# Restructuring the first tile of a six-layer cross network: x0 transposed by batch block, layer 0 begun on four accumulators

## The chip, the cores and the metric

The kernel runs on one core of a Trainium2 chip. The metric is the device time of one execution in microseconds (us), lower is better. The kernel before takes 2669.94 us (median of 4 runs, 2669.66 to 2670.76).

The engines are called PE (TensorE: matmuls and transposes), DVE (VectorE), ACT (ScalarE), POOL (GpSimd) and SP (SyncE, which issues the loads). The traces show PE at two speeds: a 512-column matmul starts every 427 ns or every 216 ns, a 128-column transpose every 107 or every 56 ns. The **gate** below is a name for this alone: it opens where the spacing falls to 216 and 56 ns (at 11.97 us in the trace of the kernel before), and it shuts where 427 and 107 ns come back. 427 beside 216 ns is called half clock.

## The reference, cut to what matters

```python
# B, Din, L = 16384, 1024, 6; all bf16
def reference(x0, ws, bs):
    x = x0
    for l in range(L):
        proj = jnp.einsum('bd,de->be', x, ws[l]) + bs[l]
        x = x0 * proj + x
    return x
```

## The kernel before

The batch is cut into 32 tiles of 512 rows. In a tile, x lies transposed (feature on the partitions). Each layer is 8 output blocks `e` of 8 matmuls over `k`, so 64 matmuls a layer and 12,288 in all. A PSUM accumulator `ps[e]` lives through all six layers; after each layer one DVE operation makes `(ps + c) * x0T`. All tiles but the first get their transposed x0 by a transposing load. In the first tile x0 is loaded as it lies, transposed on PE into PSUM and copied to `x0T` by DVE.

```python
load_x0n(0, 256)        # x0 of tile 0 in four column pieces of 256 KB (512 B rows)
load_w0(0, 128)         # layer 0's weights in column pieces
load_x0n(256, 512)
load_x0n(512, 768)
load_x0n(768, 1024)
load_w0(128, 256)
load_w0(256, 512)
load_w0(512, 1024)
for l2 in range(1, L):
    nc.sync.dma_start(out=w_sb[l2], in_=ws_v[l2])     # 2 MB each
...                      # 5 warm-up matmuls on a zeroed tile, one small transpose of bs
# first tile, first layer, e == 0
for kp in range(KT // 2):
    for k in (2 * kp, 2 * kp + 1):
        tp = psum.tile([P, NB], BF16, name="tp", tag=f"ps{1 + k % 5}")
        for bo in range(BO):                          # 4 transposes per k
            nc.tensor.transpose(tp[:, bo*P:(bo+1)*P], x0n[:, bo, k*P:(k+1)*P], ident)
        nc.vector.tensor_copy(out=x0T[:, k, :], in_=tp)
    if kp == 0:
        make_c()
    for k in (2 * kp, 2 * kp + 1):
        mm(ps[0], l, e, k, cur)                       # only block e = 0 starts here
...                      # then e = 1..7, eight matmuls each
```

Of the kernel before, what the change touches and what calls it, by code (L numbers as in the profile page):

```python
# [8 lines left out]
BF16 = mybir.dt.bfloat16  # L9
FP32 = mybir.dt.float32  # L10
ADD = mybir.AluOpType.add
MULT = mybir.AluOpType.mult

N_WARM = 5


@with_exitstack
def kernel(
    ctx: ExitStack,
    tc: tile.TileContext,  # L20
    x0: bass.AP,
    ws: bass.AP,
    bs: bass.AP,
    out: bass.AP,
):
    nc = tc.nc
    P = nc.NUM_PARTITIONS
    B, D = x0.shape
    L = ws.shape[0]
    KT = D // P  # L30
    NB = 512
    NT = B // NB
    BO = NB // P

    wpool = ctx.enter_context(tc.tile_pool(name="w", bufs=1))
    cpool = ctx.enter_context(tc.tile_pool(name="c", bufs=1))
    x0pool = ctx.enter_context(tc.tile_pool(name="x0", bufs=3))
    xpool = ctx.enter_context(tc.tile_pool(name="x", bufs=3))
    opool = ctx.enter_context(tc.tile_pool(name="o", bufs=2))
    psum = ctx.enter_context(  # L40
        tc.tile_pool(name="psum", bufs=1, space=bass.MemoryType.PSUM)
    )

    def x0_nat(t):
        return x0[t * NB : (t + 1) * NB, :].rearrange("(bo bi) d -> bi bo d", bi=P)

    def out_nat(t):
        return out[t * NB : (t + 1) * NB, :].rearrange("(bo bi) e -> bi bo e", bi=P)

    w_sb = [wpool.tile([P, KT, D], BF16, name=f"w{l}") for l in range(L)]  # L50
    ws_v = [ws[l].rearrange("(ko ki) e -> ki ko e", ki=P) for l in range(L)]

    warm = cpool.tile([P, NB], BF16, name="warm")
    nc.vector.memset(warm, 0.0)  # L54
    ident = cpool.tile([P, P], BF16, name="ident")
    make_identity(nc, ident)

    bs_nat = cpool.tile([L * KT, P], BF16, name="bs_nat")
    nc.scalar.dma_start(out=bs_nat, in_=bs.rearrange("l (eo ei) -> (l eo) ei", ei=P))

    x0n = opool.tile([P, BO, D], BF16, name="o_nat")
    x0_t0 = x0_nat(0)

    def load_x0n(c0, c1):
        nc.sync.dma_start(out=x0n[:, :, c0:c1], in_=x0_t0[:, :, c0:c1])  # L65

    def load_w0(c0, c1):
        nc.sync.dma_start(out=w_sb[0][:, :, c0:c1], in_=ws_v[0][:, :, c0:c1])  # L68

    load_x0n(0, 256)  # L70
    load_w0(0, 128)
    load_x0n(256, 512)
    load_x0n(512, 768)
    load_x0n(768, 1024)
    load_w0(128, 256)
    load_w0(256, 512)
    load_w0(512, 1024)
    for l2 in range(1, L):
        nc.sync.dma_start(out=w_sb[l2], in_=ws_v[l2])

    wps = psum.tile([P, NB], FP32, name="wps", tag="ps7")
    for _ in range(N_WARM):
        nc.tensor.matmul(  # L83
            wps, lhsT=warm[:, 0:P], rhs=warm, start=True, stop=True,
            skip_group_check=True,
        )

    bsT = psum.tile([P, L * KT], BF16, name="bsT", tag="ps6")
    nc.tensor.transpose(bsT, bs_nat, ident[: L * KT, : L * KT])  # L89
    c_sb = cpool.tile([P, L, KT], FP32, name="c_sb")  # L90

    def make_c():
        nc.vector.tensor_scalar_add(c_sb[:, 0, :], bsT[:, 0:KT], 1.0)  # L93
        for l in range(1, L):
            nc.vector.tensor_add(  # L95
                c_sb[:, l, :], c_sb[:, l - 1, :], bsT[:, l * KT : (l + 1) * KT]
            )

    def mm(ps_e, l, e, k, cur):
        nc.tensor.matmul(  # L100
            ps_e,
            lhsT=w_sb[l][:, k, e * P : (e + 1) * P],
            rhs=cur[:, k, :],
            start=(l == 0 and k == 0),
            stop=(k == KT - 1),
            skip_group_check=True,
        )

    def stt(nxt, ps_e, l, e, x0T):
        nc.vector.scalar_tensor_tensor(  # L110
            out=nxt[:, e, :],
            in0=ps_e,
            scalar=c_sb[:, l, e : e + 1],
            in1=x0T[:, e, :],
            op0=ADD,
            op1=MULT,
        )

    for t in range(NT):
        x0T = x0pool.tile([P, KT, NB], BF16, name="x0T")  # L120
        ps = [None] * KT
        cur = x0T
        if t > 0:
            nc.sync.dma_start_transpose(out=x0T, in_=x0[t * NB : (t + 1) * NB, :])
        for l in range(L):
            nxt = xpool.tile([P, KT, NB], BF16, name="xT")
            for e in range(KT):
                if l == 0:
                    if t == 0 and e == 0:
                        ps[0] = psum.tile([P, NB], FP32, name="ps0", tag="ps0")  # L130
                        for kp in range(KT // 2):
                            for k in (2 * kp, 2 * kp + 1):
                                tp = psum.tile(
                                    [P, NB], BF16, name="tp", tag=f"ps{1 + k % 5}"
                                )
                                for bo in range(BO):
                                    nc.tensor.transpose(  # L137
                                        tp[:, bo * P : (bo + 1) * P],
                                        x0n[:, bo, k * P : (k + 1) * P],
                                        ident,  # L140
                                    )
                                nc.vector.tensor_copy(out=x0T[:, k, :], in_=tp)  # L142
                            if kp == 0:
                                make_c()
                            for k in (2 * kp, 2 * kp + 1):
                                mm(ps[0], l, e, k, cur)
                        stt(nxt, ps[e], l, e, x0T)
                        continue
                    ps[e] = psum.tile([P, NB], FP32, name=f"ps{e}", tag=f"ps{e}")
                for k in range(KT):  # L150
                    mm(ps[e], l, e, k, cur)
                stt(nxt, ps[e], l, e, x0T)
            cur = nxt

        o_nat = opool.tile([P, BO, D], BF16, name="o_nat")
        n_dma = KT if t < NT - 1 else KT - 2
        for e in range(n_dma):
            nc.sync.dma_start_transpose(
                out=o_nat[:, :, e * P : (e + 1) * P], in_=cur[:, e, :]
            )  # L160
        nc.sync.dma_start(
            out=out_nat(t)[:, :, 0 : n_dma * P], in_=o_nat[:, :, 0 : n_dma * P]
        )
        if n_dma < KT:
            for i, e in enumerate(range(n_dma, KT)):
                tp = psum.tile([P, BO, P], BF16, name="tpo", tag=f"ps{i}")
                for bo in range(BO):
                    nc.tensor.transpose(  # L168
                        tp[:, bo, :], cur[:, e, bo * P : (bo + 1) * P], ident
                    )  # L170
                dst = o_nat[:, :, e * P : (e + 1) * P]
                if e == KT - 1:
                    nc.vector.tensor_copy(out=dst, in_=tp)  # L173
                else:
                    nc.scalar.copy(out=dst, in_=tp)  # L175
            nc.sync.dma_start(
                out=out_nat(t)[:, :, n_dma * P : D], in_=o_nat[:, :, n_dma * P : D]
            )
# [30 lines left out]
```

## Time and profile before

| what | value | where to read it |
|---|---|---|
| span | 2668.6 us | page, first line |
| PE busy | 100% | page, part 1 |
| full-speed matmul spacing | 216 ns | timeline, start times |
| layer 1's first matmul | 24.77 us | timeline |
| 64 matmuls of layer 0 at full speed | 13.8 us | 64 x 0.216 |

These are lines of the page of the kernel before: the chain that ended last, by engine and by line, and the costliest groups (busy us, mean ns of one, idle time before them and what ended it).

```profile
PE 100%; DMA 0%; DVE 0%; SPq 0%; issue 0%
...
L100 PE MATMUL ps<-xT,w 128*128 128x512 bf16 x10240 | 2215.3, 379 | 0.0
...
L137 PE MATMUL tp<-ident,o_nat 128*128 128x128 bf16 x32 | 4.7, 305 | 2.5 <-DMA o_nat<-in_x_dram 2.5
```

PE is the whole chain, and once the stream of matmuls runs nothing interrupts it. A restructured start can therefore win only what lies ahead of layer 1. The timeline shows that stretch. Its columns are start in us, length in us, engine, line, operation, count, and the idle time before it with its releaser; lines of PE alone are kept. (Some traces below lack a few matmul records, so a count there can be 62 where 64 ran.)

```profile
1.19 2.31 PE L83 MATMUL wps<-warm 128*128 128x512 bf16 x5 [1.19 <-DVE warm L54]
...
4.12 1.03 PE L137 MATMUL tp<-ident,o_nat 128*128 128x128 bf16 x8 [0.46 <-DMA o_nat<-in_x_dram]
...
7.20 0.40 PE L137 MATMUL tp<-ident,o_nat 128*128 128x128 bf16 x2 [2.05 <-DMA o_nat<-in_x_dram]
...
7.38 1.06 PE L100 MATMUL ps<-x0T,w 128*128 128x512 bf16 x2
...
12.22 12.71 PE L100 MATMUL ps<-x0T,w 128*128 128x512 bf16 x58
...
24.77 7.50 PE L100 MATMUL ps<-xT,w 128*128 128x512 bf16 x34
```

The first 8 transposes run at 4.12 us, then PE waits 2.05 us for the second x0 piece. The two matmuls at 7.38 us take 1.06 us to their end, so they start 427 ns apart: half clock. The 58 at 12.22 us take 12.71 us, which is 216 ns each. The gate opened at 11.97 us; that is where the trace's record of the granted clock begins. A warning about reading it: where the record has not begun, the page and the table of stretches print a clock of 1.00, so the spacing of the matmuls is the safer witness.

### The profile page before, as it was taken

To read this page: it belongs to the slowest core of one execution; us is meant where nothing else is said; L and a number is where in the kernel's file an instruction comes from. 1 tells how busy PE (TensorE), PEld (TensorE's weight loads), DVE (VectorE), ACT (ScalarE), POOL (GpSimd) and SP (SyncE) were. 2 spreads that over 40 slices of the span, in tenths; PEclk is the share of its full clock that TensorE was granted. 3 is DMA by queue.
4 is the path that set the end of the run, shared out by engine and by line. 5 is a ranking of instruction groups with operands and counts; after the bars stand their busy time and mean duration, and the time that the engine had idled before them with its cause. 6 is when DMAs were issued, how large, how long until landed. Compare 5 with 4: busy or idle time off the path is not lost.

```text
span 2668.6 us, 26965 instructions
## 1 busy us (share of the span) xinstructions
PE 2660.2 (100%) x12334; PEld 1207.0 (45%) x12334; DVE 1157.9 (43%) x1552; ACT 1.9 (0%) x2; POOL 0.7 (0%) x6
## 2 busy tenths in 40 slices
PE   9999999999999999999999999999999999999999
PEld 4444444444444444444444444444444444444444
DVE  4444444444444444444444444444444444444444
ACT  0000000000000000000000000000000000000000
POOL 0000000000000000000000000000000000000000
PEclk9999999999999999999999999999999999999999
DMA  8111011110111101111011110111101111011111
GB/s 237 48 48 31 20 46 48 48 43 9 44 48 48 48 7 42 48 48 48 9 39 48 48 48 12 36 48 48 48 14 34 48 48 48 16 32 48 32 32 28
DMA packets 295217, 114.75 MB, mean 43 GB/s; under 512 B 268992, under 2 KB 274112, under 8 KB 295104
## 3 DMA queue, kind: packets, MB, share of 16 engines
q1 hardware_dynamic: 295040, 113.02, 16.7%
q8 instruction: 96, 1.57, 0.2%
q14 instruction: 17, 0.14, 0.0%
q10 hardware_dynamic: 64, 0.01, 0.0%
HBM read 13.64 MB, written 33.55 MB: 18 GB/s over the span
## 4 chain that ended last, share of the span: by engine, by line
PE 100%; DMA 0%; DVE 0%; SPq 0%; issue 0%
PE ps L100 99%; DMA o_nat<-in_x_dram 0%; PE tp L137 0%; DVE xT L110 0%; SPq L68 0%; SPq L65 0%; DVE o_nat L173 0%; PE tpo L168 0%
## 5 line engine op out<-in xcount | busy, mean ns | idle before, releaser
L100 PE MATMUL ps<-xT,w 128*128 128x512 bf16 x10240 | 2215.3, 379 | 0.0
L100 PEld LDWEIGHTS <-w 128*128 128x128 bf16 x12288 | 1202.6, 98 | 1448.9
L110 DVE SCALAR_TENSOR_TENSOR xT<-ps,c_sb,x0T 128x512 bf16<-128x512 f32 x1536 | 1153.0, 751 | 1498.2 <-PE ps L100 1498.2
L100 PE MATMUL ps<-x0T,w 128*128 128x512 bf16 x2048 | 449.3, 380 | 0.0
L137 PE MATMUL tp<-ident,o_nat 128*128 128x128 bf16 x32 | 4.7, 305 | 2.5 <-DMA o_nat<-in_x_dram 2.5
L137 PEld LDWEIGHTS <-o_nat 128*128 128x128 bf16 x32 | 3.6, 141 | 4.6 <-DMA o_nat<-in_x_dram 2.9
L142 DVE COPY x0T<-tp 128x512 bf16<-128x512 bf16 x8 | 3.4, 425 | 4.9 <-PE tp L137 4.9
L83 PE MATMUL wps<-warm 128*128 128x512 bf16 x5 | 2.3, 629 | 1.2 <-DVE warm L54 1.2
L175 ACT ACT_TABLE_LOAD x1 | 1.3, 1283 | 2505.2 <-DMA out_dram<-o_nat 2505.2
L83 PEld LDWEIGHTS <-warm 128*128 128x128 bf16 x5 | 0.6, 134 | 2.0 <-DVE warm L54 1.2
L168 PE MATMUL tpo<-ident,xT 128*128 128x128 bf16 x8 | 0.8, 220 | 0.6 <-DVE xT L110 0.6
L93 DVE TENSOR_SCALAR c_sb<-bsT 128x8 f32<-128x8 bf16 x1 | 0.2, 167 | 2.6 <-PE bsT L89 2.6
L168 PEld LDWEIGHTS <-xT 128*128 128x128 bf16 x8 | 0.5, 98 | 1.0 <-DVE xT L110 0.8
L95 DVE TENSOR_TENSOR c_sb<-c_sb,bsT 128x8 f32<-128x8 f32 x5 | 0.8, 158 | 0.1
L175 ACT COPY o_nat<-tpo 128x512 bf16<-128x512 bf16 x1 | 0.6, 586 | 157.0 <-PE tpo L168 157.0
L54 DVE MEMSET warm<- 128x256 uint32 x1 | 0.3, 272 | 0.9 <-PEq L193 0.9
L173 DVE COPY o_nat<-tpo 128x512 bf16<-128x512 bf16 x1 | 0.4, 425 | 0.5 <-PE tpo L168 0.5
L89 PEld LDWEIGHTS <-bs_nat 48*128 48x128 bf16 x1 | 0.1, 100 | 0.8 <-DMA bs_nat<-in_bs_dram 0.8
masks.py:199 POOL TENSOR_SCALAR_AFFINE_SELECT ident<-ident 128x128 bf16<-128x128 bf16 x1 | 0.3, 294 | 0.1
L89 PE MATMUL bsT<-ident,bs_nat 48*128 48x48 bf16 x1 | 0.2, 218 | 0.0
masks.py:197 POOL MEMSET ident<- 128x128 bf16 x1 | 0.2, 205 | 0.3 <-POOLq L193 0.3
L193 POOL MEMSET const-bfloat16-1.0<- 128x1 bf16 x1 | 0.1, 102 | 0.0
(3 smaller groups left out, 0.3 us busy)
## 6 DMA issues: line engine op xcount, KB each, us to landing
out_dram<-o_nat SPq DMA_DIRECT2D x31, 1024.0 KB, 6.0
w<-in_ws_dram SPq DMA_DIRECT2D x5, 2048.0 KB, 19.5
o_nat<-xT SPq DMA_TRANSPOSE x254, 2.4
o_nat<-in_x_dram SPq DMA_DIRECT2D x4, 256.0 KB, 5.5
w<-in_ws_dram SPq DMA_DIRECT2D x1, 1024.0 KB, 8.3
out_dram<-o_nat SPq DMA_DIRECT2D x1, 768.0 KB, 3.6
w<-in_ws_dram SPq DMA_DIRECT2D x2, 256.0 KB, 5.1
w<-in_ws_dram SPq DMA_DIRECT2D x1, 512.0 KB, 7.2
```

The lines of the kernel that those rows point to most:

```text
L54: nc.vector.memset(warm, 0.0)
L83: nc.tensor.matmul(wps, lhsT=warm[:, 0:P], rhs=warm, start=True, stop=True, skip_group_check=True,)
L89: nc.tensor.transpose(bsT, bs_nat, ident[: L * KT, : L * KT])
L93: nc.vector.tensor_scalar_add(c_sb[:, 0, :], bsT[:, 0:KT], 1.0)
L95: nc.vector.tensor_add(c_sb[:, l, :], c_sb[:, l - 1, :], bsT[:, l * KT : (l + 1) * KT])
L100: nc.tensor.matmul(ps_e, lhsT=w_sb[l][:, k, e * P : (e + 1) * P], rhs=cur[:, k, :], start=(l == 0 and k == 0), stop=(k == KT - 1), skip_gr ...
L110: nc.vector.scalar_tensor_tensor(out=nxt[:, e, :], in0=ps_e, scalar=c_sb[:, l, e : e + 1], in1=x0T[:, e, :], op0=ADD, op1=MULT,)
L137: nc.tensor.transpose(tp[:, bo * P : (bo + 1) * P], x0n[:, bo, k * P : (k + 1) * P], ident,)
L142: nc.vector.tensor_copy(out=x0T[:, k, :], in_=tp)
L168: nc.tensor.transpose(tp[:, bo, :], cur[:, e, bo * P : (bo + 1) * P], ident)
L173: nc.vector.tensor_copy(out=dst, in_=tp)
L175: nc.scalar.copy(out=dst, in_=tp)
```

## The change

The intent is to have PE transpose each batch block of x0 as it lands (four loads with 2 KB rows), and then to run half of layer 0, four output blocks, with `k` outermost, so that each transposed `k` feeds four matmuls. The warm-up reads a constant that exists already, so it starts earlier and has six matmuls. The weights' first half comes in quarters.

```diff
-N_WARM = 5
+N_WARM = 6
-    load_x0n(0, 256)
-    load_w0(0, 128)
-    load_x0n(256, 512)
 ... (the other column loads go too)
+    for bo in range(BO):
+        nc.sync.dma_start(out=x0n[:, bo, :], in_=x0_t0[:, bo, :])
+    for kp in range(KT // 2):
+        nc.sync.dma_start(
+            out=w_sb[0][:, 2 * kp : 2 * kp + 2, 0:H],
+            in_=ws_v[0][:, 2 * kp : 2 * kp + 2, 0:H],
+        )
+    nc.sync.dma_start(out=w_sb[0][:, :, H:D], in_=ws_v[0][:, :, H:D])
 ... (warm-up matmuls read constant ones in place of a zeroed tile)
+                        for bo in range(BO - 1):
+                            for k in range(KT):
+                                tr(k, bo)
+                        tr_last(0)           # last block's transposes and the copies
+                        tr_last(2)
 ...
+                        for k in range(KT):
+                            if k % 2 == 0 and k + 4 < KT:
+                                tr_last(k + 4)
+                            for e2 in range(EH):            # EH = 4
+                                mm(ps[e2], l, e2, k, cur)
+                        for e2 in range(EH):
+                            stt(nxt, ps[e2], l, e2, x0T)
```

In the built program the scheduler puts all 32 transposes ahead of the first matmul.

More of the change, by code (lines that the diff above doesn't have):

```diff
@@ L51 @@
     ws_v = [ws[l].rearrange("(ko ki) e -> ki ko e", ki=P) for l in range(L)]
-    warm = cpool.tile([P, NB], BF16, name="warm")
-    nc.vector.memset(warm, 0.0)
     ident = cpool.tile([P, P], BF16, name="ident")
@@ L62 @@
     x0_t0 = x0_nat(0)
-    def load_x0n(c0, c1):
-        nc.sync.dma_start(out=x0n[:, :, c0:c1], in_=x0_t0[:, :, c0:c1])
-    def load_w0(c0, c1):
-        nc.sync.dma_start(out=w_sb[0][:, :, c0:c1], in_=ws_v[0][:, :, c0:c1])
-    load_x0n(0, 256)
-    load_w0(0, 128)
-    load_x0n(256, 512)
-    load_x0n(512, 768)
-    load_x0n(768, 1024)
-    load_w0(128, 256)
-    load_w0(256, 512)
-    load_w0(512, 1024)
+    H = D // 2
+    for bo in range(BO):
[6 more added lines that the diff above has]
+    nc.sync.dma_start(out=w_sb[0][:, :, H:D], in_=ws_v[0][:, :, H:D])
     for l2 in range(1, L):
         nc.sync.dma_start(out=w_sb[l2], in_=ws_v[l2])
-    wps = psum.tile([P, NB], FP32, name="wps", tag="ps7")
+    wps = psum.tile([P, NB], FP32, name="wps", tag="ps2")
+    ones_w = nc.const_aps.tensor(1.0, [P, P], BF16)
+    ones_x = nc.const_aps.tensor(1.0, [P, NB], BF16)
     for _ in range(N_WARM):
         nc.tensor.matmul(
-            wps, lhsT=warm[:, 0:P], rhs=warm, start=True, stop=True,
+            wps, lhsT=ones_w, rhs=ones_x, start=True, stop=True,
             skip_group_check=True,
         )
-    bsT = psum.tile([P, L * KT], BF16, name="bsT", tag="ps6")
+    bsT = psum.tile([P, L * KT], BF16, name="bsT", tag="ps3")
     nc.tensor.transpose(bsT, bs_nat, ident[: L * KT, : L * KT])
@@ L128, with tr, tr_last @@
                 if l == 0:
-                    if t == 0 and e == 0:
-                        ps[0] = psum.tile([P, NB], FP32, name="ps0", tag="ps0")
-                        for kp in range(KT // 2):
-                            for k in (2 * kp, 2 * kp + 1):
-                                tp = psum.tile(
-                                    [P, NB], BF16, name="tp", tag=f"ps{1 + k % 5}"
-                                )
-                                for bo in range(BO):
-                                    nc.tensor.transpose(
-                                        tp[:, bo * P : (bo + 1) * P],
-                                        x0n[:, bo, k * P : (k + 1) * P],
-                                        ident,
-                                    )
-                                nc.vector.tensor_copy(out=x0T[:, k, :], in_=tp)
-                            if kp == 0:
-                                make_c()
-                            for k in (2 * kp, 2 * kp + 1):
-                                mm(ps[0], l, e, k, cur)
-                        stt(nxt, ps[e], l, e, x0T)
+                    if t == 0 and e < KT // 2:
+                        if e > 0:
+                            continue
+                        EH = KT // 2
+                        make_c()
+                        tps = [
+                            psum.tile(
+                                [P, 2, NB], BF16, name=f"tp{kp}", tag=f"ps{EH + kp}"
+                            )
+                            for kp in range(KT // 2)
+                        ]
+                        def tr(k, bo):
+                            nc.tensor.transpose(
+                                tps[k // 2][:, k % 2, bo * P : (bo + 1) * P],
+                                x0n[:, bo, k * P : (k + 1) * P],
+                                ident,
+                            )
+                        def tr_last(k):
+                            tr(k, BO - 1)
+                            tr(k + 1, BO - 1)
+                            for k2 in (k, k + 1):
+                                nc.vector.tensor_copy(
+                                    out=x0T[:, k2, :], in_=tps[k2 // 2][:, k2 % 2, :]
+                                )
+                        for bo in range(BO - 1):
[4 more added lines that the diff above has]
+                        for e2 in range(EH):
+                            ps[e2] = psum.tile(
+                                [P, NB], FP32, name=f"ps{e2}", tag=f"ps{e2}"
+                            )
+                        for k in range(KT):
[3 more added lines that the diff above has]
+                                mm(ps[e2], l, e2, k, cur)
+                        for e2 in range(EH):
+                            stt(nxt, ps[e2], l, e2, x0T)
```

## The prediction

> **What bounds the kernel now.** TensorE (PE). The page shows PE busy 100% and the chain of waits is 99% layer matmuls. The timeline shows them starting every 215.9 ns; 12,288 of them are 2,653 us of the 2,668.6 us span. No other engine or DMA queue bounds the steady state, and the change leaves it alone. Only the start can move: layer 1's first matmul starts at 24.77 us (timeline), while layer 0's 64 matmuls need 64 x 0.2159 = 13.8 us. So 10.95 us is start-up. The tail after the last matmul (5.5 us) is untouched.
>
> **Where the 10.95 us goes (timeline).** The first x0 piece lands at 4.07 us. PE then does 8 transposes, one each 107 ns, and waits 2.05 us for the second x0 piece (7.15 us). After that it runs 24 transposes and 8 matmuls without idling, but matmuls start 427 ns apart and transposes 107 ns apart until about 11.97 us, where the granted-clock record begins; then 216 and 56 ns. [...]
>
> **What the change does.**
> - x0 comes as four 2 KB-row pieces ahead of any weight. Packets in the trace: 512 B take 28 ns, 1,024 B 48, 2,048 B 84. So 256 KB in 2 KB rows takes about 0.67 us instead of 0.9. The first load's fixed part is about 2.4 us (12 KB of bs: 2.44 us from issue to landing). Estimate: landings at 3.8, 4.5, 5.2, 5.9 us; weight quarters (1 KB rows, 0.77 us each) at 6.6 to 9.0; second half of w0 near 12; w1 near 17.5.
> - PE: 6 warm matmuls instead of 5, starting about 0.3 us earlier (no memset), ending near 3.5 us; then 32 transposes by batch block, all ahead of the first matmul, then 32 matmuls k-outer over four accumulators, each k (0.86 us) covering two copies (0.425 us each), so DVE keeps up.
> - Adds nothing to PE but one warm matmul, hidden behind the first landing. Four evictions (0.75 us) come in a burst; layer 1 needs them 7 us later.
>
> **On the critical path.** The 2 us DMA gap goes; slow-clock time shrinks because PE is nearly continuously busy from 0.9 us. Two cases:
> - gate opens near 5.2 us: transposes finish with the last x0 piece, first real matmul about 6.8, layer 1 about 20.6; gain 4.1 us.
> - gate opens near 8.6 us: transposes end 7.2, first matmul 7.3 at 427 ns, layer 1 about 21.8; gain 3.0 us.
> Even odds, less 0.2 us for late landings (the trace has a slow DMA spell near 4 to 5 us): gain 3.3 us.
>
> **Predicted time: 2666.6 us, 8 in 10 between 2665.2 and 2668.4.** Faster by over 2%: 0.005; within 2%: 0.99; slower by over 2%: 0.005.
>
> **What would show it.** Timeline: layer 1's first matmul at 20.6 to 21.8 us; all x0 landed by about 6 us; PE gaps over 0.3 us gone after 4 us; start spacing 216 ns from between 5 and 8.6 us; steady spacing and tail unchanged; w1 landed before layer 1.
>
> **What would make it wrong.** The gate opening only near 12 us again (gain about 1.5); x0 or the first weight quarter landing over 1 us late, so PE idles; evictions in a burst stalling layer 1; a different gate phase in each run.

The two opening times of the cases, 5.2 and 8.6 us, stand as assumptions. The terms of the sum are all there: the mean of 4.1 and 3.0 us, less 0.2, put down as 3.3 us.

## The result, and the profile after

The changed kernel takes 2667.73 us (median of 9 runs, 2667.23 to 2669.68) beside 2669.94 us (13 runs, 2669.02 to 2671.03). The ratio is 0.9993, with a 95% interval of 0.9984 to 1.0002. Ratios here are the mean time of one kernel's runs over that of the other's in the same rounds, so they are not quite the ratio of the quoted medians. By the 2% rule the two are the same. The interval of the ratio holds 1 in every comparison of this document, so what follows rests on traces and on how the runs lie.

The profiled runs of the two kernels took 2670.76 and 2667.53 us, 3.23 us apart. The first is the highest of the four runs at hand before the change, 0.82 us over their median, so this pair shows more than the 2.21 us between the medians. The timeline of the changed kernel shows where (same columns as above).

```profile
0.78 2.72 PE L79 MATMUL wps<-const-bfloat16-1.0 128*128 128x512 bf16 x6 [0.78 <-PEq L213]
...
3.58 1.37 PE L138 MATMUL tp<-ident,o_nat 128*128 128x128 bf16 x16
...
5.45 0.62 PE L138 MATMUL tp<-ident,o_nat 128*128 128x128 bf16 x8 [0.50 <-DMA o_nat<-in_x_dram]
...
6.91 0.62 PE L138 MATMUL tp<-ident,o_nat 128*128 128x128 bf16 x8 [0.84 <-DMA o_nat<-in_x_dram]
7.24 2.74 DVE L148 COPY x0T<-tp 128x512 bf16<-128x512 bf16 x8 [2.41 <-PE tp L138]
...
7.71 13.97 PE L96 MATMUL ps<-x0T,w 128*128 128x512 bf16 x64 [0.18 <-DVE x0T L148]
...
21.52 10.74 PE L96 MATMUL ps<-xT,w 128*128 128x512 bf16 x49
```

The 64 matmuls now run without a break and at full speed, and layer 1 starts at 21.52 us, 3.25 us earlier. But the first real matmul starts at 7.71 us, **0.33 us later** than before (7.38). The same shows in the page's groups:

```profile
L96 PE MATMUL ps<-xT,w 128*128 128x512 bf16 x10240 | 2215.4, 379 | 0.0
...
L138 PE MATMUL tp<-ident,o_nat 128*128 128x128 bf16 x32 | 2.6, 237 | 1.3 <-DMA o_nat<-in_x_dram 1.3
```

The steady stream did not change (2215.3 and 2215.4 us). The transposes' busy time fell from 4.7 to 2.6 us, at the same count: most of them ran at full clock.

A ledger makes this exact. In every trace the span minus the start of layer 1 is 2643.9 us, so the whole difference between kernels lies ahead of layer 1. That start is the first real matmul, plus 13.82 us for 64 matmuls, plus 0.056 us for each transpose that stands between them, plus what the slow clock and waits add:

| trace | gate opens (us) | last x0 piece lands | first real matmul | transposes after it | slow clock and waits after it | layer 1 starts |
|---|---|---|---|---|---|---|
| before | 11.97 | 8.97 | 7.38 | 22: 1.23 | 2.34 | 24.77 |
| after | 4.25 | 6.87 | 7.71 | 0 | 0 | 21.52 |

So the 3.25 us are 2.34 us of slow clock, plus 1.23 us of transposes that no longer stand between matmuls, less 0.33 us of later start. PE's waits for x0 shrank from 2.5 to 1.3 us (the two groups of transposes above), but the first real matmul, which now stands behind all 32 transposes, came no earlier. The slow-clock term agrees with an estimate from the spacings: PE was busy at half clock from 7.2 to 11.97 us, and at 427 ns in place of 216 about half of that time, 4.77 x 0.5 = 2.4 us, is lost.

The last x0 piece landed at 6.87 us, where the prediction had 5.9. The view of the transfers cuts 2 to 7 us into 40 slices; first the kernel before:

```profile
GB/s 8 12 154 168 219 309 336 318 316 305 307 301 289 293 289 305 279 244 207 178 180 188 238 283 291 303 254 262 254 262 246 258 320 324 320 324 297 297 307 307
```

and the changed kernel:

```profile
GB/s 180 49 0 328 410 360 442 361 459 377 442 360 377 197 328 279 393 197 311 328 377 360 147 148 197 172 229 287 279 279 262 246 344 279 279 311 344 361 312 279
```

The changed kernel moves 360 to 459 GB/s at 2.5 to 3.5 us and 384 to 388 from 13.6 us on (table of stretches), but 147 to 287 from 4.75 to 6 us. In the same spell of both kernels single packets take up to 0.9 us (changed) and 1.4 us (before), where the medians are 84 ns (2 KB) and 27 ns (512 B). I call it the slow spell. The packet records, in which the first tile's x0 can be told by its 2 KB, show that a few packets come late and not the whole stream: of the 512 packets of x0, 500 had ended by 5.74 us, near the predicted 5.9, but the last one at 6.51 us, when 250 packets of weights had ended too. In e1 below the same times are 5.98 and 7.48 us. In both traces the landing follows that last packet by 0.36 us.

### The profile page after: what moved, and what is told of

It is laid out like the page before. It is cut to its first block, busy times and chain, and to the rows that moved or that the text cites. A ratio compares the mean times of both kernels' runs of the same rounds, so it can differ in the third digit from the quotient of the medians.

```text
span 2665.4 us, 26968 instructions
## 1 busy us (share of the span) xinstructions
PE 2658.3 (100%) x12335; PEld 1205.8 (45%) x12335; DVE 1157.1 (43%) x1551; ACT 1.9 (0%) x2; POOL 0.7 (0%) x6
## 4 chain that ended last, share of the span: by engine, by line
PE 100%; DMA 0%; DVE 0%; SPq 0%; issue 0%
PE ps L96 100%; DMA o_nat<-in_x_dram 0%; SPq L65 0%; DVE xT L106 0%; DVE x0T L148 0%; DVE o_nat L193 0%; PE tpo L188 0%; PE tp L138 0%
## 5 line engine op out<-in xcount | busy, mean ns | idle before, releaser
L96 PE MATMUL ps<-xT,w 128*128 128x512 bf16 x10240 | 2215.4, 379 | 0.0
```

What stands on the lines that cost most here:

```text
L96: nc.tensor.matmul(ps_e, lhsT=w_sb[l][:, k, e * P : (e + 1) * P], rhs=cur[:, k, :], start=(l == 0 and k == 0), stop=(k == KT - 1), skip_gr ...
```

## The experiments

Each of the 12 runs was profiled and timed in five rounds against the kernel before; all results were correct. Jobs ran on different chips, so a run is compared with those of its own job. Layer 1's start, the gate and landings are of the one profiled run; the medians are of five runs. The theories:

- **A**: the change wins mostly because PE's gate opens earlier, and the spread between runs is the moment at which it opens, which differs from run to run.
- **B** (rival, for the spread): late landings of x0 make it.
- **C** (rival, for the gain): the new order of loads, transposes and accumulators is what wins.
- **D**: the change starts its first real matmul no earlier because a whole megabyte of x0 and a weight quarter must land first.

### e1, e8, e10: the changed kernel again

No edit.

> The changed kernel unaltered, for the spread and a second trace. Theory A (the clock gate of TensorE is what the change mostly wins on[...]): runs fall into an early group near 2667.2 to 2667.8 us (gate open between 4.2 and 5.0 us) and a late group of 2668.5 us and more (a trace of such a run shows matmuls 427 ns apart after 7.7 us, or the gate closing in the waits at 5 and 6 us). Rival B (the landing of the x0 pieces makes the spread): every trace has the gate open before 5.5 us and the late runs have the last x0 piece landing 1 to 2 us later. Median 2667.7 under both.

> The changed kernel again, beside the other three on the same chip. By theory A its time is that of the gate: a trace with the gate open once for good by 5 us gives 2667.2 to 2668 us, one in which it closes again in the waits gives 2669 us or more.

> The changed kernel beside e9 on the same chip: 2667.5 to 2669.5 us, by the gate; its last x0 block lands at 6.8 to 7.9 us.

Measured: 2669.25 us (2667.98 to 2670.78) beside 2670.03; 2667.94 (2667.57 to 2669.90) beside 2669.74; 2667.68 (2667.35 to 2668.77) beside 2669.77. The median of 2667.7 us that I expected of e1 under both theories was missed by 1.5 us. The traces differ:

| trace | gate | x0 pieces land | first real matmul | slow clock and waits after it | layer 1 |
|---|---|---|---|---|---|
| e1 | open 4.66 to 8.07, shut to 11.49 | 3.58, 4.21, 5.74, 7.84 | 8.69 | 1.35 | 23.86 |
| e8 | open from 6.55 | 3.68, 4.30, 5.68, 7.78 | 8.63 | 0 | 22.44 |
| e10 | open from 5.03 | 3.52, 4.16, 5.65, 6.99 | 7.84 | 0 | 21.65 |

In e1 the gate opened and shut again. Its timeline, PE alone:

```profile
5.79 0.62 PE L138 MATMUL tp<-ident,o_nat 128*128 128x128 bf16 x8 [0.62 <-DMA o_nat<-in_x_dram]
...
7.89 0.90 PE L138 MATMUL tp<-ident,o_nat 128*128 128x128 bf16 x8 [1.48 <-DMA o_nat<-in_x_dram]
...
8.69 15.34 PE L96 MATMUL ps<-x0T,w 128*128 128x512 bf16 x62
...
23.86 0.38 PE L96 MATMUL ps<-xT,w 128*128 128x512 bf16 x1
```

and its table of stretches (us, then busy time of PE, its weight loads, DVE, ACT and POOL, then the granted clock, DMA share and GB/s):

```profile
6.80:10.20 3.40, 2.31 (x12) 1.29 (x13) 1.99 (x6) 0.00 (x0) 0.00 (x0) 0.69 1.03 351
10.20:13.60 3.40, 3.35 (x13) 1.42 (x13) 0.75 (x3) 0.00 (x0) 0.00 (x0) 0.81 1.08 371
```

The granted clock of 0.69 and 0.81 is the shut stretch, 8.07 to 11.49 us. The transposes at 7.89 us straddle it, 0.90 us in place of 0.62. Both A and B are right in part: the traces of the later runs (e1, e8) have a late or shut gate **and** a late last piece, and in e1 the wait for that piece, 1.48 us, is most of the 2.1 us that PE was idle between the gate's opening at 4.66 us and its shutting at 8.07. B as I put it (the gate open in every trace, landings alone) is refuted by e1; A alone is not enough, as e8 lost 0.9 us against the first trace with no slow matmul at all, by a last piece that landed 0.9 us later. My expectation for e8 tied the time to the gate alone: its profiled run took 2668.45 us with the gate open at 6.55, a case that it did not foresee.

Over all 25 runs of the changed kernel the mean is 2668.33 us and the median 2667.94; the 40 runs of the kernel before in the same rounds have 2669.91 and 2669.87. The gain is 1.6 us on average over the chips, and 3.2 us in the lucky pair of traces.

### e2 and e12: the kernel before, with PE kept busy in its wait

```diff
-N_WARM = 5
+N_WARM = 6
+N_FILL = 6
 ...
                             if kp == 0:
                                 make_c()
+                                for _ in range(N_FILL):
+                                    with tc.issue_after(last.ins):
+                                        last = warm_mm()     # idle matmul, result unused
```

The transposes and the first two matmuls are pinned behind these too, as the scheduler otherwise moves the idle matmuls to the front. The pin also moved a few transposes past matmuls. Loads and accumulation are as before.

> The kernel before, with six idle matmuls after the first 8 transposes (in the 2.05 us wait for the second x0 piece) and a sixth warm-up matmul; loads, transposes and accumulation as before. Theory A: the gate opens between 4.6 and 8.0 us instead of 11.97, the first real matmul stays near 7.2 to 7.6, and layer 1 starts near 22.5 us instead of 24.77: about 2.2 us gained, 2667.8 us, though nothing of the change's restructuring is in it. Rival C (the gain comes from the order of loads and transposes and from the four interleaved accumulators): no gain, 2669.9 us, or a loss by the idle work.

> The kernel before with idle matmuls in its wait, again, beside e11 on the same chip: 2668.3 us as in e2, layer 1 near 22.3 us, spread under 1 us.

Measured: 2668.29 us (2667.83 to 2668.54) and 2668.49 us (2668.00 to 2668.70), beside 2670.03 and 2669.66. The mean of the ten runs is 2668.34 us, that of the changed kernel's 25 runs 2668.33; but these means mix chips. Against the kernel before in the same job, by medians, the filled kernel gains 1.7 and 1.2 us, the changed kernel 2.2 (first result), 0.8 (e1), 1.8 (e8) and 2.1 us (e10). The timeline of e2:

```profile
4.84 2.31 PE L85 MATMUL wps<-warm 128*128 128x512 bf16 x6
...
7.00 0.59 PE L105 MATMUL ps<-x0T,w 128*128 128x512 bf16 x2
...
9.75 12.71 PE L105 MATMUL ps<-x0T,w 128*128 128x512 bf16 x56
...
22.30 1.89 PE L105 MATMUL ps<-xT,w 128*128 128x512 bf16 x8
```

The gate opened at 6.57 us (5.13 in e12), and layer 1 starts at 22.30 (22.01). Beside the first trace of the kernel before, e2's layer 1 starts 2.47 us earlier; in the ledger 2.20 of these are slow clock (2.34 down to 0.14). Six matmuls that compute nothing, and one more warm-up matmul, bring the old structure to about the changed kernel's average, with a quarter of its spread (0.9 us over ten runs, 3.6 over 25). Rival C in its plain form, no gain without the restructuring, falls.

The two parts of this edit were not tested apart. The kernel before waits 0.46 us ahead of its first transposes (4.12 us), and its gate opened at 11.97. The sixth warm-up matmul fills that wait, and the idle matmuls begin only at about 4.8 us, so for e12's opening at 5.13 us it alone may have been enough; ahead of e2's opening at 6.57 us most of the six idle matmuls had started as well.

### e3: the changed kernel without its warm-up

```diff
-N_WARM = 6
+N_WARM = 0
```

> The changed kernel without its six warm-up matmuls. Theory A: [...] 1.6 to 3.4 us of the gain are lost: 2669.3 to 2671.1 us, no better than before. Rival C: the warm-up is of no weight to a stream that starts at 7.7 us anyway; 2667.7 to 2668 us.

Measured: 2669.75 us (2669.13 to 2670.37) beside 2670.03 for the kernel before. The timeline of e3, PE alone:

```profile
7.77 1.03 PE L138 MATMUL tp<-ident,o_nat 128*128 128x128 bf16 x8 [1.26 <-DMA o_nat<-in_x_dram]
...
8.68 15.61 PE L96 MATMUL ps<-x0T,w 128*128 128x512 bf16 x62
```

The gate opened at 12.47 us, the first real matmul started at 8.68, the slow clock cost 1.84 us, and layer 1 started at 24.34. The restructured kernel without warm-up is back at the old time, as A expected. But the changed kernel in the same job (e1) is only 0.5 us faster by the median, its range (2667.98 to 2670.78) holds all of e3's, and layer 1 starts only 0.48 us earlier in its trace, so e3 fits A without proving it. (The last x0 piece landed at 7.72 us here, about as in e1.)

### e4 and e11: the changed kernel with idle matmuls in its two waits

```diff
+FILL = (0, 3, 4)          # e11: (0, 1, 2)
 ...
                         for bo in range(BO - 1):
                             for k in range(KT):
                                 tr(k, bo)
+                            for _ in range(FILL[bo]):
+                                warm_mm()            # pinned in this place
```

> The changed kernel with three idle matmuls after the second and four after the third batch block's transposes, in its two waits for x0 (0.50 and 0.84 us). Theory A: PE has no gap[...]; the late group goes; median 2667.3 to 2667.6 us, highest under 2668.2. Rival B: spread as in the changed kernel itself (highest 2669 to 2669.7), since loads are the same.

> The changed kernel with one and two idle matmuls in its two waits for x0 instead of three and four, which in e4 ran up to 0.6 us past the landing. If the restructuring is worth something of its own once the gate is no matter, layer 1 starts at 21.5 to 21.9 us and the median is 0.4 to 0.8 us under e12's; if all of the change's gain was the gate, the two are within 0.2 us.

Measured: e4 2668.27 us (2667.97 to 2668.59), e11 2667.92 us (2667.06 to 2668.98). In e4 the spread fell from 2.8 us (e1, same job) to 0.6, as A said, but the median is no better than e2's (2668.29, same job), and my 2667.3 to 2667.6 was missed. The trace says why: the gate opened only at 6.25 us, so the first three idle matmuls, from 5.31 us, ran mostly at 427 ns and put off the third block's transposes to 6.42 us (its piece had landed at 4.99); the other four, at full speed, then held PE until 7.75 us, when the last transposes began, though the last piece had landed at 7.10. With fewer of them (e11) the gate opened at 6.75, the last transposes began 0.04 us after the landing (7.26), the first real matmul came at 8.11 and layer 1 at 21.91. By the numbers set down before the run this is the case in which the restructuring is worth something of its own: against e12 in its job the median is 0.57 us lower. But the ranges overlap and the two traces differ by only 0.10 us. Whether the restructuring wins anything of its own once the gate is taken care of stays unclear; by the medians of these two pairs it is between nothing and 0.6 us.

### e6 and e7: what delays the last piece of x0

```diff
 # e6: blocks 1 and 3 from ACT's queue
-        nc.sync.dma_start(out=x0n[:, bo, :], in_=x0_t0[:, bo, :])
+        (nc.sync, nc.scalar)[bo % 2].dma_start(out=x0n[:, bo, :], in_=x0_t0[:, bo, :])
```

```diff
 # e7: column pieces of 512 B rows in place of batch blocks, transposes in that order
-        nc.sync.dma_start(out=x0n[:, bo, :], in_=x0_t0[:, bo, :])
+        c0, c1 = 2 * bo * P, 2 * (bo + 1) * P
+        nc.sync.dma_start(out=x0n[:, :, c0:c1], in_=x0_t0[:, :, c0:c1])
```

> The changed kernel with x0 blocks 1 and 3 issued by ScalarE's queue instead of SyncE's. If the late landing of the last x0 block (6.9 to 7.8 us against 5.9 predicted) comes from the issue or order on one queue, the last block lands by 6 us and layer 1 comes about 1 us earlier than in the changed kernel at the same gate times. If it is a slow spell of the memory side at 4 to 6 us, it lands as late as before and the time is that of the changed kernel.

> The changed kernel with x0 loaded in four column pieces (512 B rows, as before) in place of batch blocks (2 KB rows), transposes in the order in which these land. If the 2 KB rows bring the last x0 data earlier, as predicted (0.67 against 0.9 us a piece), the last piece lands about 0.9 us later here and the time is 0.9 us longer than the changed kernel's. If a slow spell sets the last landing, it is the same within 0.5 us.

Measured, in one job with e8:

| run | median us | x0 pieces land | gate opens | first real matmul | layer 1 |
|---|---|---|---|---|---|
| e8, the changed kernel | 2667.94 | 3.68, 4.30, 5.68, 7.78 | 6.55 | 8.63 | 22.44 |
| e6, two queues | 2669.05 | 3.47, 5.43, 4.80, 7.22 | 10.03 | 8.18 | 22.89 |
| e7, 512 B rows | 2670.83 | 3.95, 4.77, 7.26, 8.07 | 13.30 | 9.67 | 25.26 |

A second queue does not bring the last piece to 6 us, and the 7.22 us lie within the 6.87 to 7.84 us of the changed kernel's four traces. Its median is 1.1 us over e8's, with overlapping ranges; in its trace the slow clock after the first real matmul costs 0.89 us. So this one trace shows nothing won by the second queue. With 512 B rows the last piece comes 0.3 us after e8's, not 0.9, so in this pair the row length sets little of the landing; the changed kernel's own four traces differ by 1.0 us, so the pair can't settle it. The piece that is hit differs: the third in e7, the fourth in the changed kernel. The timeline of e7, PE alone:

```profile
3.99 1.65 PE L139 MATMUL tp<-ident,o_nat 128*128 128x128 bf16 x12 [0.35 <-DMA o_nat<-in_x_dram]
...
7.30 2.49 PE L139 MATMUL tp<-ident,o_nat 128*128 128x128 bf16 x20 [1.66 <-DMA o_nat<-in_x_dram]
...
9.67 15.75 PE L97 MATMUL ps<-x0T,w 128*128 128x512 bf16 x62
```

PE waits 1.66 us with the gate still shut, does 20 transposes at half clock, and sees the gate open at 13.30 us. The median is longer by 2.9 us (the ranges overlap: 2668.24 to 2671.31 beside 2667.57 to 2669.90), layer 1 in the traces by 2.82 us, of which 1.77 are slow clock after the first real matmul. From 3.40 to 6.80 us PE was busy for 3.12 us in e8, whose gate opened in that stretch, and for 1.88 us in e7, whose gate did not. So in these two traces the 2 KB rows go with a different *shape* of the wait and an earlier gate; that the one made the other is the author's reading, and these two traces do not show it. What the slow spell is, no run here shows. Packets of over 0.3 us start between 4 and 6 us in all 14 traces (2 to 18 in each), with both queues and both row lengths, though every trace has some at other times too.

### e5 and e9: column pieces with four and with six accumulators

By theory D the first matmuls need only 512 KB: one column piece of x0 and its weights. Candidate e5 loads column pieces and weight quarters in turn, keeps the change's four accumulators, has a seventh warm-up matmul, and does 8 transposes ahead of the first matmul. The first two of the eight `k` then give 8 matmuls.

```diff
-    for bo in range(BO):
-        nc.sync.dma_start(out=x0n[:, bo, :], in_=x0_t0[:, bo, :])
     for kp in range(KT // 2):
+        c0, c1 = 2 * kp * P, 2 * (kp + 1) * P
+        nc.sync.dma_start(out=x0n[:, :, c0:c1], in_=x0_t0[:, :, c0:c1])
         nc.sync.dma_start(...)           # weight quarter, as in the change
 ...
+                        tr_pair(0)       # 8 transposes, 2 copies
+                        for k in range(KT):
+                            for e2 in range(EH):
+                                if k % 2 == 1 and e2 == EH // 2 and k + 1 < KT:
+                                    tr_pair((k + 1) // 2)
+                                pin(mm(ps[e2], l, e2, k, cur))
```

> A candidate: the four accumulators of the change, but x0 comes in the column pieces of before, each followed by its weight quarter, and only 8 transposes stand ahead of the first matmul; 7 warm-up matmuls. Theory D (the change started its first real matmul no earlier than before because all of x0, 1 MB, and a weight quarter must land first; 512 KB would do): first real matmul at 5.0 to 5.6 us, layer 1 at 20.5 to 21.8 us, 2666.4 to 2667.5 us, and a small spread as PE has no long wait. If instead the late third or fourth load (1.5 to 2 us after the one ahead of it in all traces so far) hits the second x0 piece, PE waits near 6 to 7 us and layer 1 comes at 22 us or later.

Measured: 2667.69 us (2667.59 to 2669.47), beside 2667.94 for the changed kernel in the same job (e8). The first real matmul started at 5.45 us, 2.3 us earlier than in the changed kernel's first trace, as theory D has it, but layer 1 at 21.99: 0.45 us earlier than in e8's trace, and 0.47 later than in the first. The expected 20.5 to 21.8 us was missed; the case of a late second piece came true. That piece landed at 7.34 us, after the slow spell, where the first had landed at 3.92. PE lost 0.65 us there and about 0.25 us at each of three places where transposes stood too close ahead of the matmuls that need their copy. Starting early was worth little here, as the work at hand ran out.

Candidate e9, also with seven warm-up matmuls, gives the early stretch more work: six accumulators (12 matmuls for each pair of `k`; the program's other two PSUM buffers, ps6 and ps7, take the transposes in turn), transposes further ahead of their use, two idle matmuls before the first copy is ready, and the last pair of `k` block by block so that DVE's evictions do not bunch.

```diff
+    EH = 6
+    H = EH * P
 ...
+                        for k in range(KT - 2):
+                            for e2 in range(EH):
+                                if k % 2 == 1 and e2 == (2 if k == 1 else 0):
+                                    tr_pair((k + 1) // 2)
+                                pin(mm(ps[e2], l, e2, k, cur))
+                        for e2 in range(EH):
+                            for k in range(KT - 2, KT):
+                                pin(mm(ps[e2], l, e2, k, cur))
+                            stt(nxt, ps[e2], l, e2, x0T)
```

> A candidate made from the column pieces: six accumulators in place of four, so that the first x0 piece and the first six eighths of its weights give 12 matmuls (2.6 us) of work before the second x0 piece, which the slow spell of the loads delays to about 7.3 us, is needed; two idle matmuls cover the wait for the first copies. Theory D with the slow spell: first real matmul near 5.4 us, no wait of PE over 0.3 us after it, layer 1 at 20.7 to 21.3 us if the gate is open by 5 us and at most 1.5 us later if it is not: 2666.5 to 2667.5 us, and in any case under the changed kernel of the same rounds. Rival: PE was not waiting for x0 but for weights (which come later here, 384 KB at a time), and layer 1 comes at 22 us or later.

Measured: 2666.76 us (2666.61 to 2667.35), beside 2667.68 us (2667.35 to 2668.77) for the changed kernel (e10) and 2669.77 for the kernel before. The timeline of e9, PE alone:

```profile
4.00 0.71 PE L144 MATMUL tp<-ident,o_nat 128*128 128x128 bf16 x8
...
5.44 1.89 PE L103 MATMUL ps<-x0T,w 128*128 128x512 bf16 x8 [0.29 <-DVE x0T L151]
...
7.17 0.61 PE L144 MATMUL tp<-ident,o_nat 128*128 128x128 bf16 x8
...
9.77 0.61 PE L144 MATMUL tp<-ident,o_nat 128*128 128x128 bf16 x8
...
12.81 0.61 PE L144 MATMUL tp<-ident,o_nat 128*128 128x128 bf16 x8
...
20.59 3.62 PE L103 MATMUL ps<-xT,w 128*128 128x512 bf16 x16
```

After 5.44 us no line carries a wait: 5.44 + 13.82 + 24 x 0.056 = 20.60, and layer 1 starts at 20.59. The second piece landed at 5.88 us here, before it was needed, so this trace doesn't show the slow spell being covered; and the gate opened at 4.23 us, as early as in the change's first trace, so it doesn't show a late gate being covered either. Its run is the fastest of the five. That weights would hold PE up, the rival in its expectation, is not seen. The several parts of this edit were not tested apart. What the runs show is that the slowest of e9's five is no slower than the fastest of the changed kernel's five beside it. It is the best of the kernels here, 3.0 us under the kernel before (medians) and 0.9 us under the change: 0.1% of the time.

## Why the prediction was right, point by point

- **The time.** 2666.6 us was predicted with a range of 2665.2 to 2668.4; 2667.73 us was measured on the first chip. The range held. The centre was 1.1 us too low, of which 0.8 is a slip of base: the gain of 3.3 us was read off a trace whose run took 2670.76 us, but was taken from the median, 2669.94. From the trace's own run it gives 2667.5, and the changed kernel's profiled run took 2667.53. In the later job e1 the median, 2669.25 us, lay outside the range.
- **What bounds the kernel, and that only the start can move.** Right: the span after layer 1's start is 2643.9 us in all traces.
- **Layer 1's start between 20.6 and 21.8 us, for a gain of 3.0 to 4.1 us.** Right for the first pair of traces (21.52 us, gain 3.25) and for e10 (21.65); too early for e8 (22.44) and e1 (23.86). That the first trace lies so near the mean of the two cases, 21.2 us plus 0.2 for late landings, is in part luck: the first real matmul came 0.46 us later than their mean of 7.05 plus 0.2, and the slow clock cost nothing where the mean of the cases holds 0.35. The two errors nearly cancel. On average the gain was 1.6 us.
- **The first step that failed: "all x0 landed by about 6 us".** The term was sized by a steady 0.67 us a piece, with 0.2 us for the slow spell. By the packet records that size held for the bulk of x0 (500 of 512 packets by 5.74 us in the first trace) and failed for the last few packets, on which the landing hangs. The last piece landed at 6.87, 7.84, 7.78 and 6.99 us in the four traces of the changed kernel. So "the 2 us DMA gap goes" failed too: PE still waits 1.1 to 2.1 us after 4 us, mostly split in two, and the first real matmul came at 7.7 to 8.7 us, not 6.8 to 7.3.
- **The second step that failed: two gate cases at even odds.** I took the gate to open once, at 5.2 or 8.6 us, times that no trace at hand showed. The moment varies: the gate opened at 4.25, 4.66, 5.03 and 6.55 us in four traces of the same kernel, and in e1 it shut again, a case that I had not counted. The spread of this moment (there called the gate phase) stood in the list of what could make it wrong. It shows in e1; in the first trace the gate opened so early that no real matmul was slow, so there the late landings alone moved layer 1.
- **"Slow-clock time shrinks because PE is nearly continuously busy".** Right, and the larger part of the gain in the profiled pair: 2.34 of 3.25 us. Experiment e2 supports it (the gate at 6.57 us in place of 11.97, and 2.20 of its 2.47 us), with the sixth warm-up matmul and the idle ones not told apart; e3 fits it, but its difference from e1 is within the spread.
- **DVE keeps up; the burst of evictions does no harm; the weights are early.** Right: the copies start 0.33 us apart against 0.86 us for four matmuls, nothing waits at layer 1, and its weights landed at 18.05 us.

## What to carry to other kernels

Before restructuring a start, write the ledger: when the first useful matmul starts, what stands between the useful ones, and what the slow clock costs; here one more warm-up matmul and idle matmuls in one wait matched, on average, a rewritten first tile. A load order that lets work begin early pays only with enough work per byte to last until the next piece, which e5 (8 matmuls a piece) and e9 (12, with the transposes further ahead of their use) suggest. And when a kernel's runs spread by 2 us, take several traces before explaining a median: against one trace of the kernel before, one trace of the changed kernel showed a gain of 3.2 us and another of 0.9. A gain read off a trace must also be taken from that trace's own run and not from the median.

## What these traces show of the gate and the loads

- In e1 no gap was over 1.5 us, yet the gate, open from 4.66 us, shut at 8.07; in between PE had transposes alone and was idle for 0.62 and 1.48 us, 2.1 us together. In the first trace of the changed kernel the gate, open from 4.25 us, stayed open with waits of 0.50, 0.84 and 0.18 us (1.5 together), and in e5 with 0.69 and 0.49 us (1.2). That the idle time shut the gate is the reading of one shutting; no run here tests it.
- In the kernel before the gate opened at 11.97 us, 4.77 us after PE's last wait had ended (7.20). In e8 it opened at 6.55 us, and between the last warm-up matmul and the opening PE had transposes alone (of x0, and one of bs). So in that trace no matmul of layer 0 was needed to open it.
- In e1 the record of the granted clock fits the spacing of the matmuls (open to 8.07 us, shut to 11.49); but in no trace does a record stand before the first opening, where the views print 1.00 at matmuls 427 ns apart.
- The loads had a slow spell early in the kernel: 147 to 287 GB/s at 4.75 to 6 us, after 360 to 459 at 2.5 to 3.5 us and before 384 to 388 from 13.6 us on (after), with single packets of up to 1.4 us (before). Only the last few packets of x0 came late: 500 of x0's 512 had ended by 5.74 us, the last at 6.51 us (after). Its cause is open.
